# Sigmoid attention and hypermixer: stores by token group over 128 partitions, and the last column half in two PSUM banks

## The chip, the cores and the metric

The kernel runs on one core of a Trainium2 chip. TensorE (PE) multiplies matrices and writes PSUM; VectorE (DVE) and ScalarE (ACT) read PSUM and write SBUF; GpSimd (POOL) works on SBUF alone; SyncE (SP) issues nearly all DMA transfers, which 16 DMA engines carry out. The metric is the time of one execution on the device, in microseconds; lower is better.

## What is computed

```python
# q, k, v: (8 sequences, 12 heads, 448 tokens, 64), float32
scores = scale * q @ k.T - log(448)
attn   = 1 / (1 + exp(-scores))              # sigmoid, no softmax
x      = (attn @ v), heads side by side      # (8, 448, 768)
wq, wk = x @ w_q, x @ w_k                    # (8, 448, 64) each
W_tok  = scale * wq @ wk.T                   # tokens by tokens
out    = relu(W_tok @ x) @ w_out             # (8, 448, 768), float32
```

## The kernel before

The attention of a sequence is done in three groups ("quads") of four heads, so there are 24 quads. A quad's q, k and v are loaded in float32 (448 KB each), cast to bfloat16 mostly by POOL, transposed by DVE or by TensorE, and multiplied: scores on TensorE, sigmoid on ACT (L331), values on TensorE, a copy to SBUF on DVE (L355). After three quads the sequence goes through the token mixer, whose last product with w_out gives rows of the output. A string written out by hand, PLAN, sets the order of all steps; its letters S and P are scores and values, O and o a part of an output block, D lets one waiting block of output be stored. A second string, BANKS, names for each step the PSUM bank or pair of banks that it takes: PSUM has eight banks, in four pairs numbered 0 to 3.

Token t of a sequence is numbered t = 7 p + i, p from 0 to 63 and i from 0 to 6. A token group is one i: 64 tokens, which lie 7 rows apart in the output. Each row of the output has 768 floats, in two column halves of 384.

Output is made in three ways, by the pair w of sequences to which it belongs.

- `out_chunk`, for w = 0 and 1: 128 partitions hold two token groups, 64 partitions each, all 768 columns. The store (L649 to L652) is two transfers, one for each half of the partitions: 64 partitions, 3072 bytes each, 192 KB.
- `out_pair`, for w = 2 and 3, one sequence at a time: partitions 0 to 63 hold the first column half and partitions 64 to 127 the second one, of token groups k and k + 4, which stand side by side in the tile `o` as `o[:, 0]` and `o[:, 1]`. The store (L604 to L610) is two transfers, one for each half of the partitions, that is for each column half: 64 partitions, 2 x 1536 bytes each, 192 KB. The block of w = 2 that holds the middle group of both sequences goes out in four transfers of 32 partitions (L612 to L616).
- `middle`, for the middle group (i = 3) of the two sequences of w = 3, which is the last block of the program: partitions 0 to 63 are the one sequence's tokens, 64 to 127 the other's. Its four parts are the first and the second three of the six blocks of the sum, for column half 0 and then for column half 1. Each column half has one bank of a pair; when it is complete, DVE copies its columns 0 to 191 and then ACT its columns 192 to 383 (L555), out of the same bank. ACT's copy waits for DVE's. Half 0 is stored in one transfer, half 1 in two of 64 partitions, on SP's queue and on ACT's (L559).

SP issues its transfers in program order. Each transfer raises one of eight counters, in turn, when it has landed, and the next one on the same counter waits for that; so at most eight are under way. The float32 loads share six buffers (`lds`, tiles ld), and a load waits until the cast of what lay there before is done. The output blocks of w = 0, 1 and most of w = 2 lie in five buffers of their own (tile o); the last ones use the six load buffers, when no load is left.

Of the kernel before, what the change touches and what calls it, by code (L numbers as in the profile page):

```python
# [17 lines left out]
def kernel(  # L18
# [12 lines left out]
    nc = tc.nc  # L31
    B, H, S, HD = q.shape
    D = H * HD
# [3 lines left out]
    NI, NP = 7, 64  # L37
    NU = B
    NJ = H // 4
    NC = D // P  # L40
    NB = D // 2
    HALF = (slice(0, 64), slice(64, 128))
# [5 lines left out]
    def pool(name, bufs, **kw):  # L48
# [20 lines left out]
        "021012h01210321g201321g2h01gh201g20132cd302c302302131e301230"  # L69
        "ef310ef3102102c302d320d320123cd20gh120g102310g102hg102312gh1"  # L70
        "0210ef130210ef1302120120320312321031021021321a31032032132012"
        "0123020210320120c3210210312"
    )
    given = list("".join(BANKS))
    held = set()
# [1 line left out]
    def bank2():  # L77
        n = int(given.pop(0))
        assert not held & {2 * n, 2 * n + 1}
        held.update({2 * n, 2 * n + 1})  # L80
        return n, pairs[n], pairs16[n]

    def bank1():
        b = "abcdefgh".index(given.pop(0))
        assert b not in held
        held.add(b)
        return "abcdefgh"[b], pairs[b // 2][:, b % 2], pairs16[b // 2][:, b % 2]

    def release(fb):
        gone = {2 * fb, 2 * fb + 1} if isinstance(fb, int) else {"abcdefgh".index(fb)}  # L90
        assert gone <= held
        held.difference_update(gone)

    wout16 = singles.tile([P, 2 * NC, D], BF16, name="wout16")
# [14 lines left out]
    def ld_next():  # L109
        nld[0] += 1  # L110
        return lds[(nld[0] - 1) % 6]
# [8 lines left out]
    def mm(*args, **kw):  # L120
        products.append(nc.tensor.matmul(*args, **kw))  # L121
# [6 lines left out]
    COPY = dict(v=nc.vector.tensor_copy, s=nc.scalar.copy, g=nc.gpsimd.tensor_copy)  # L128
# [387 lines left out]
    ot = {}  # L516
# [4 lines left out]
    def flush(n=None):  # L521

        for _, f in stores[:n]:
            f()
        del stores[:n]

    def o_tile(shape):

        while stores and stores[0][0] <= o_tiles[0] - 5:
            flush(1)  # L530
        o_tiles[0] += 1
        return p_o.tile(shape, F32, tag="o", name="o")

    def slot(half, b):

        return b // 2 + (0 if b % 2 == half else NC)

    def middle(w, us, k, part, fb, ps):

        x = part // 2  # L540
        for c in range(part % 2 * NC // 2, (part % 2 + 1) * NC // 2):
            for u in us:
                st = mxs[w].rearrange("p (c u s) -> p c u s", u=2, s=S)[:, c, u, 3 * NP : 4 * NP]
                mm(
                    ps[HALF[u], x, 0:NB], st, wout16[:, c, x * NB : (x + 1) * NB],
                    start=(c == 0), stop=(c == NC - 1),
                )
        if part % 2:
            if not x:
                ot[0] = ld_next()[:, 0:D]  # L550
            o = ot[0][:, x * NB : (x + 1) * NB]
            half = NB // 2
            for y in range(2):
                cols = slice(y * half, (y + 1) * half)
                COPY["vs"[y]](out=o[:, cols], in_=ps[:, x, cols])  # L555
            rows = out[2 * w : 2 * w + 2].rearrange("u (p i) d -> (u p) i d", i=NI)[:, NI // 2, x * NB : (x + 1) * NB]
            if x:
                for y in range(2):
                    (nc.sync, nc.scalar)[y].dma_start(out=rows[HALF[y]], in_=o[HALF[y]])  # L559
            else:  # L560
                nc.sync.dma_start(out=rows, in_=o)
        if part < 3:
            opened.append((w, us, k, part + 1, fb, ps))
        else:
            release(fb)

    def out_pair(act, tail):

        if opened:
            w, us, k, part, fb, ps = opened.pop()  # L570
        else:
            w, us, k = chunks.pop(0)
            part = 0
            fb, ps, _ = bank2()
        if len(us) == 2 and w == MIXED:
            middle(w, us, k, part, fb, ps)
            return
        mx = mxs[w].rearrange("p (b s) -> p b s", b=12)
        at = S // 2 - 32 if len(us) == 2 else k * NP + (32 + S // 2 if us[0] else 0)
        for b in range(3 * part, 3 * part + 3):  # L580
            for y in range(2):
                st = mx[HALF[y], b, at : at + NP]
                if w == MIXED:
                    j = (b - b % 2) * S + us[0] * S + (b % 2) * 4 * NP + k * NP
                    st = mxs[w][HALF[y], j : j + NP]
                for x in range(2):
                    mm(
                        ps[HALF[x], y, 0:NB], st, wout16[HALF[y], slot(y, b), x * NB : (x + 1) * NB],
                        start=(b == 0), stop=(b == 11),
                    )  # L590
        if part < 3:
            opened.append((w, us, k, part + 1, fb, ps))
            return
        late = len(cast) == len(ORDER) + 2
        ends = w == NU // 2 - 1 and us[-1] and len(chunks) < 2
        o = ld_next()[:, 0:D].rearrange("p (b x) -> p b x", b=2) if late else o_tile([P, 2, NB])
        if ends:
            for y in range(2):
                COPY["vs"[y]](out=o[:, y], in_=ps[:, y, 0:NB])
        else:  # L600
            COPY["s" if act else "v"](out=o, in_=ps[:, :, 0:NB])
        release(fb)

        def store():  # L604
            for x in range(2):
                cols = slice(x * NB, (x + 1) * NB)
                if len(us) == 1:
                    (nc.scalar if ends and x else nc.sync).dma_start(
                        out=out[2 * w + us[0]].rearrange("(p i) d -> p i d", i=NI)[:, k : k + 5 : 4, cols], in_=o[HALF[x]],
                    )  # L610
                    continue
                for u in us:  # L612
                    nc.sync.dma_start(
                        out=out[2 * w + u].rearrange("(r n i) d -> i n r d", r=2, i=NI)[NI // 2, :, :, cols],
                        in_=o[64 * x + 32 * u : 64 * x + 32 * u + 32],
                    )  # L616

        stores.append((o_tiles[0] - 1, store))
        if tail or late:
            flush()  # L620

    def out_chunk(act, tail):

        if opened:
            w, m, nb, fb, ps = opened.pop()
            part = 1
        else:
            w, m, nb = chunks.pop(0)
            if nb < 0:
                nb = 0  # L630
                chunks.insert(0, (w, m, 1))
            fb, ps, _ = bank1()
            part = 0
        if nb == 0 and not part:
            ot[0] = o_tile([P, D])
        o = ot[0]
        ps = ps if part else ps[:, 0:NB]
        for c in range(part * NC // 2, (part + 1) * NC // 2):
            mm(
                ps, mxs[w][:, 2 * S * c + m * P : 2 * S * c + (m + 1) * P],  # L640
                wout16[:, c, nb * NB : (nb + 1) * NB], start=(c == 0), stop=(c == NC - 1),
            )
        if not part:
            opened.append((w, m, nb, fb, ps))
            return
        COPY["s" if act else "v"](out=o[:, nb * NB : (nb + 1) * NB], in_=ps)  # L646
        release(fb)

        def store():  # L649
            for y in range(2):  # L650
                b, i = divmod(2 * m + y, NI)
                nc.sync.dma_start(out=out[2 * w + b].rearrange("(p i) d -> p i d", i=NI)[:, i], in_=o[HALF[y]])  # L652

        if nb:
            stores.append((o_tiles[0] - 1, store))
# [23 lines left out]
    def cols(r):  # L679
        return slice(r.start * HD, r.stop * HD)  # L680
# [8 lines left out]
        out=ident, in_=ident, compare_op=ALU.not_equal, fill=1.0, base=0,  # L689
# [93 lines left out]
    for t16, t32, r, e in (  # L783
# [3 lines left out]
            out=t16[:, r].rearrange("p i b d -> p b i d"),  # L787
            in_=t32[:, :, cols(r)].rearrange("p b (i d) -> p b i d", d=HD),
# [3 lines left out]
    def tr_part(nm, t16, r, e, tiled=False):  # L792
# [19 lines left out]
        out=k016[:, K3].rearrange("p i b d -> p b i d"), in_=k0[:, :, cols(K3)].rearrange("p b (i d) -> p b i d", d=HD),  # L812
# [10 lines left out]
    for t in PLAN:  # L823
        pump_loads()
        pump()
        if t in "EF":
            fb, ps, _ = bank2()
# [13 lines left out]
        c = done[kind]  # L841
# [4 lines left out]
        elif kind == "P":  # L846
            n, i = divmod(c, NI)
# [15 lines left out]
        elif t == "z":  # L863
            n = quads_r.pop(0)
# [12 lines left out]
        elif kind == "C":  # L877
            for y in range(2):
                nc.sync.dma_start(
                    out=wout16[HALF[y], NC + 2 * c : NC + 2 * c + 2, :], in_=wout16[HALF[1 - y], 2 * c : 2 * c + 2, :],  # L880
# [5 lines left out]
        elif kind == "M":  # L886
            u, x = divmod(c, NC // 2)
# [42 lines left out]
```

## Time and profile before

| | |
|---|---|
| median of 3 runs (lowest, highest) | 185.74 us (184.32, 186.18) |
| the profiled execution's own time | 185.85 us |
| its span, first to last instruction | 184.1 us |
| mean granted TensorE clock | 0.995 |
| bytes read from HBM, written | 35.78 MB, 11.01 MB |
| first and last output transfer issued | 69.97 us, 180.45 us |
| last TensorE work on the chain ends | 179.68 us |

How to read it: a busy share is the part of the span in which an engine had an instruction under way. In the windows, the column after the granted clock (PEclk) is the mean busy share of the 16 DMA engines, and the last one the GB/s that they moved. SPq and ACTq are the issues of transfers from SP's and ACT's queue; the time of an issue is that of the queue, not of the transfer. The chain of waits is followed back from the last instruction, at each step to what released it.

### The profile page before, as it was taken

How to read it: one execution, taken by the hardware profiler on the slowest of the kernel's cores; microseconds unless marked ns; L12 is line 12 of the kernel's file. 1: busy time of each engine (PE TensorE's matmuls, PEld its weight loads, DVE VectorE, ACT ScalarE, POOL GpSimd, SP SyncE). 2: the span in 40 equal slices, each digit the busy share in tenths (PEclk: the TensorE clock that was granted, in tenths of full speed). 3: DMA queues.
4: the chain of work that ended last, by engine and by line, in shares of the span. 5: the costliest groups of instructions: out<-in, count | busy, mean ns of one | idle time of the engine just before them, and what ended most of it. 6: DMA issues, size and time to landing. Idle time of an engine off the chain costs nothing.

```text
span 184.1 us, 8404 instructions
## 1 busy us (share of the span) xinstructions
PE 171.2 (93%) x3618; PEld 112.3 (61%) x3618; DVE 134.0 (73%) x205; ACT 159.9 (87%) x207; POOL 117.0 (64%) x156
## 2 busy tenths in 40 slices
PE   7987778799999999999999999999999999999990
PEld 7544434454564655565656556456778898888970
DVE  2445679988999898988848877689785894694310
ACT  4699998999999999998998999999989979974330
POOL 1445696999799996799999937999999400000000
PEclk9999999999999999999999999999999999999998
DMA  5999999968999768999979998998992343432686
GB/s 176 370 382 283 305 356 333 394 244 267 400 395 390 226 215 272 353 270 366 338 199 309 313 335 271 325 391 286 303 313 65 90 111 90 109 90 66 148 223 172
DMA packets 24261, 48.51 MB, mean 264 GB/s; under 512 B 3872, under 2 KB 16416, under 8 KB 24224
## 3 DMA queue, kind: packets, MB, share of 16 engines
q1 hardware_dynamic: 24000, 47.69, 79.3%
q8 instruction: 28, 0.46, 1.0%
q10 hardware_dynamic: 224, 0.30, 0.6%
q14 instruction: 9, 0.07, 0.1%
HBM read 35.78 MB, written 11.01 MB: 254 GB/s over the span
## 4 chain that ended last, share of the span: by engine, by line
PE 80%; DVE 5%; ACT 5%; issue 3%; POOL 2%; DMA 2%; SPq 0%; ACTq 0%; POOLq 0%
PE banks L121 76%; PE banks L124 4%; ACT at L331 4%; DMA ld<-in_moe_w_k_dram 2%; DVE xt L355 1%; POOL wqk L754 1%; DVE qk L251 1%; POOL qk L211 1%; DVE qk L264 1%; DVE mx L469 1%; POOL v L221 0%; DVE k L221 0%; DVE xn L384 0%; DVE wqk L429 0%; ACT qk L801 0%
## 5 line engine op out<-in xcount | busy, mean ns | idle before, releaser
L331 ACT ACTIVATE at<-banks 128x896 bf16<-128x896 f32 x168 | 141.6, 940 | 6.6 <-PE banks L121 6.1
L121 PE MATMUL banks<-wout,mx 64*64 64x384 bf16 (+2 forms) x816 | 66.2, 324 | 0.7 <-issue 0.6
L121 PE MATMUL banks<-qk 64*64 64x448 bf16 x672 | 60.8, 358 | 4.2 <-ACT at L331 2.7
L121 PEld LDWEIGHTS <-mx 64*64 64x64 bf16 (+2 forms) x816 | 39.5, 105 | 17.5 <-issue 7.1
L211 POOL CAST qk<-ld 128x896 bf16<-128x896 f32 x38 | 44.6, 1193 | 8.4 <-issue 7.2
L121 PE MATMUL banks<-at,v 64*64 64x448 bf16 x672 | 46.7, 350 | 1.5 <-POOL v L221 0.8
L121 PEld LDWEIGHTS <-qk 64*64 64x64 bf16 x672 | 26.6, 105 | 24.8 <-issue 18.0
L355 DVE CAST xt<-banks 128x896 bf16<-128x896 f32 x23 | 25.0, 1086 | 7.6 <-PE banks L121 5.8
L121 PEld LDWEIGHTS <-v 64*64 64x64 bf16 x672 | 23.3, 106 | 7.5 <-issue 1.5
L469 DVE TENSOR_SCALAR mx<-banks 128x896 bf16<-128x896 f32 (+1 forms) x21 | 19.9, 955 | 5.0 <-PE banks L121 4.2
L221 POOL CAST v<-ld 128x896 bf16<-128x896 f32 x22 | 20.3, 930 | 1.2 <-DMA ld<-in_v_dram 0.6
L271 DVE STREAM_TRANSPOSE qk<-qk 128x448 f32<-128x448 f32 x26 | 16.0, 629 | 0.1
L251 DVE STREAM_TRANSPOSE qk<-qk 32x448 f32<-32x448 f32 x24 | 15.3, 636 | 0.6
L384 DVE COPY xn<-banks 128x896 bf16<-128x896 bf16 x21 | 13.1, 624 | 3.6 <-PE banks L124 2.6
L170 POOL COPY qk<-qk 32x448 uint32<-32x448 uint32 x26 | 14.4, 554 | 1.6
L173 POOL COPY qk<-swap 32x448 uint32<-32x448 uint32 x26 | 14.4, 554 | 1.5
L121 PE MATMUL banks<-xt,wqk 64*64 64x448 bf16 (+1 forms) x84 | 13.8, 353 | 0.2 <-ACT at L331 0.2
L646 DVE COPY o<-banks 128x384 f32<-128x384 f32 x17 | 9.4, 553 | 3.4 <-PE banks L121 3.0
L124 PEld LDWEIGHTS <-xt 64*64 64x64 bf16 (+1 forms) x588 | 9.8, 108 | 3.1 <-issue 1.6
L124 PE MATMUL banks<-ident,xt 64*64 64x64 bf16 (+1 forms) x588 | 10.4, 194 | 0.2
L121 PE MATMUL banks<-wqk,tmp 64*64 64x448 bf16 (+3 forms) x72 | 8.7, 291 | 0.0
L121 PE MATMUL banks<-wq,tmp 64*64 64x448 bf16 (+2 forms) x72 | 8.4, 292 | 0.0
(67 smaller groups left out, 136.1 us busy)
## 6 DMA issues: line engine op xcount, KB each, us to landing
ld<-in_q_dram SPq DMA_DIRECT2D x24, 448.0 KB, 6.1
ld<-in_v_dram SPq DMA_DIRECT2D x24, 448.0 KB, 5.9
ld<-in_k_dram SPq DMA_DIRECT2D x23, 448.0 KB, 5.9
out_dram<-o SPq DMA_DIRECT2D x38, 192.0 KB, 4.9
out_dram<-ld SPq DMA_DIRECT2D x14, 192.0 KB, 3.0
ld<-in_moe_w_out_dram SPq DMA_DIRECT2D x6, 384.0 KB, 5.3
wout<-wout SPq DMA_DIRECT2D x6, 192.0 KB, 5.7
out_dram<-o SPq DMA_DIRECT2D x4, 96.0 KB, 1.9
```

The source lines that it names most:

```text
L121: products.append(nc.tensor.matmul(*args, **kw))
L124: products.append(nc.tensor.transpose(*args, **kw))
L170: eng.tensor_copy(out=w[lo, 1], in_=w[hi, 0])
L173: eng.tensor_copy(out=w[hi, 0], in_=z[lo])
L211: COPY[e](out=f[:, :, "qk".index(nm)].rearrange("p e i d y -> p e y i d"), in_=ld.pop((nm, n)).rearrange("p (y i e d) -> p e y i d", y=2, ...
L221: COPY[e](out=t16.rearrange("p i b d -> p b i d"), in_=ld.pop((nm, n)).rearrange("p b (i d) -> p b i d", i=NI),)
L251: nc.vector.transpose(out=qk[n][other : other + 32, h].rearrange("p t i n -> p (t i n)").bitcast(F32), in_=w[own : own + 32, 1 - h],)
L271: nc.vector.transpose(out=qk[n][:, t].rearrange("p t i n -> p (t i n)").bitcast(F32), in_=w)
L331: nc.scalar.activation(dst, src, ACTF.Sigmoid, bias=attn_bias, scale=attn_scale)
L355: COPY[eng](out=xt(u, j), in_=ps)
L384: COPY[eng](out=xn, in_=ps)
L469: nc.vector.tensor_scalar(dst, ps, moe_scale, 0.0, ALU.mult, ALU.max)
```

## The change

Four things change.

- `out_chunk`: where both token groups of a block belong to the same sequence, one transfer of 128 partitions and 384 KB stores it. The pattern of its destination has the token group outermost (2), then the tokens (64), then 768 columns. One block in seven has its two groups in different sequences; its two transfers stay.
- `out_pair`, one sequence at a time: the two transfers are now one for each token group, `o[:, 0]` and `o[:, 1]`, each of 128 partitions and 192 KB. The pattern of the destination has the column half outermost (2), then the tokens (64), then 384 columns.
- `middle`: column half 0 is copied by DVE alone. Column half 1 is made as two pieces of 192 columns, each over all six blocks of the sum, in the two banks of another pair (number 0, the one added to BANKS). DVE copies the first piece, ACT the second. The transfers of the block are the same.
- In the last but one block, each of the two stores needs one of the two copies (DVE's for `o[:, 0]`, ACT's for `o[:, 1]`), where each needed both.

```diff
--- before.py
+++ after.py
@@ -69,7 +69,7 @@
         "021012h01210321g201321g2h01gh201g20132cd302c302302131e301230"
         "ef310ef3102102c302d320d320123cd20gh120g102310g102hg102312gh1"
         "0210ef130210ef1302120120320312321031021021321a31032032132012"
-        "0123020210320120c3210210312"
+        "0123020210320120c32102103120"
     )
     given = list("".join(BANKS))
     held = set()
@@ -537,32 +537,35 @@
 
     def middle(w, us, k, part, fb, ps):
 
-        x = part // 2
-        for c in range(part % 2 * NC // 2, (part % 2 + 1) * NC // 2):
+        if part < 2:
+            begin, n, cs = 0, NB, range(part * NC // 2, (part + 1) * NC // 2)
+        else:
+            begin, n, cs = (part * NB // 2, NB // 2, range(NC))
+        if part == 2:
+            release(fb)
+            fb, ps, _ = bank2()
+        for c in cs:
             for u in us:
                 st = mxs[w].rearrange("p (c u s) -> p c u s", u=2, s=S)[:, c, u, 3 * NP : 4 * NP]
                 mm(
-                    ps[HALF[u], x, 0:NB], st, wout16[:, c, x * NB : (x + 1) * NB],
+                    ps[HALF[u], part // 3, 0:n], st, wout16[:, c, begin : begin + n],
                     start=(c == 0), stop=(c == NC - 1),
                 )
-        if part % 2:
-            if not x:
-                ot[0] = ld_next()[:, 0:D]
-            o = ot[0][:, x * NB : (x + 1) * NB]
-            half = NB // 2
-            for y in range(2):
-                cols = slice(y * half, (y + 1) * half)
-                COPY["vs"[y]](out=o[:, cols], in_=ps[:, x, cols])
-            rows = out[2 * w : 2 * w + 2].rearrange("u (p i) d -> (u p) i d", i=NI)[:, NI // 2, x * NB : (x + 1) * NB]
-            if x:
-                for y in range(2):
-                    (nc.sync, nc.scalar)[y].dma_start(out=rows[HALF[y]], in_=o[HALF[y]])
-            else:
-                nc.sync.dma_start(out=rows, in_=o)
+        if not part:
+            ot[0] = ld_next()[:, 0:D]
+        o = ot[0]
+        if part:
+            COPY["s" if part == 3 else "v"](out=o[:, begin : begin + n], in_=ps[:, part // 3, 0:n])
+        cols = slice(0, NB) if part < 2 else slice(NB, D)
+        rows = out[2 * w : 2 * w + 2].rearrange("u (p i) d -> (u p) i d", i=NI)[:, NI // 2, cols]
+        if part == 1:
+            nc.sync.dma_start(out=rows, in_=o[:, cols])
         if part < 3:
             opened.append((w, us, k, part + 1, fb, ps))
-        else:
-            release(fb)
+            return
+        for y in range(2):
+            (nc.sync, nc.scalar)[y].dma_start(out=rows[HALF[y]], in_=o[HALF[y], cols])
+        release(fb)
 
     def out_pair(act, tail):
 
@@ -602,13 +605,14 @@
         release(fb)
 
         def store():
+            if len(us) == 1:
+                for y in range(2):
+                    (nc.scalar if ends and y else nc.sync).dma_start(
+                        out=out[2 * w + us[0]].rearrange("(p i) (x c) -> i x p c", i=NI, x=2)[k + 4 * y], in_=o[:, y],
+                    )
+                return
             for x in range(2):
                 cols = slice(x * NB, (x + 1) * NB)
-                if len(us) == 1:
-                    (nc.scalar if ends and x else nc.sync).dma_start(
-                        out=out[2 * w + us[0]].rearrange("(p i) d -> p i d", i=NI)[:, k : k + 5 : 4, cols], in_=o[HALF[x]],
-                    )
-                    continue
                 for u in us:
                     nc.sync.dma_start(
                         out=out[2 * w + u].rearrange("(r n i) d -> i n r d", r=2, i=NI)[NI // 2, :, :, cols],
@@ -647,6 +651,10 @@
         release(fb)
 
         def store():
+            b, i = divmod(2 * m, NI)
+            if i + 1 < NI:
+                nc.sync.dma_start(out=out[2 * w + b].rearrange("(p i) d -> i p d", i=NI)[i : i + 2], in_=o)
+                return
             for y in range(2):
                 b, i = divmod(2 * m + y, NI)
                 nc.sync.dma_start(out=out[2 * w + b].rearrange("(p i) d -> p i d", i=NI)[:, i], in_=o[HALF[y]])
```

In what follows a row is one instruction, or several alike with their count; for a transfer the numbers are the counts of the destination's pattern, the outermost first. Names: ld_101 and the like are load buffers, o a block of output, wout_83 the bfloat16 weights, banks PSUM.

SP's queue at the first stores of output, at 70 us of the span before:

```order
 L197 DMA ld_102<-in_v_dram 128x2x448
-L652 DMA out_dram<-o 64x768 x4
-L879 DMA wout_83<-wout_83 64x1536 x2
-L652 DMA out_dram<-o 64x768 x2
+L656 DMA out_dram<-o 2x64x768 x2
+L887 DMA wout_83<-wout_83 64x1536 x2
+L656 DMA out_dram<-o 2x64x768
 L189 DMA ld_103<-in_k_dram 128x896
 L189 DMA ld_104<-in_q_dram 128x896
```

Nothing changes its place: six stores of 64 partitions become three of 128, ahead of the same two loads, and the outermost count goes from 64 to 2.

SP's queue where the output blocks change from `out_chunk` to `out_pair` (from 130 us before). Before:

```order
L652 DMA out_dram<-o 64x768 x6
L608 DMA out_dram<-o 64x2x384 x6
L613 DMA out_dram<-o 32x2x384 x4
L608 DMA out_dram<-o 64x2x384 x4
L608 DMA out_dram<-ld_101 64x2x384 x2
```

After, the same place:

```order
L656 DMA out_dram<-o 2x64x768 x3
L610 DMA out_dram<-o 2x64x384 x6
L617 DMA out_dram<-o 32x2x384 x4
L610 DMA out_dram<-o 2x64x384 x4
L610 DMA out_dram<-ld_101 2x64x384 x2
```

The transfers stand in the same order; the stores by token group are as many as those by column half were, with 2 outermost in place of 64.

ACT's queue at the end of the program:

```order
-L599 COPY ld_101<-banks 128x384
-L608 DMA out_dram<-ld_101 64x2x384
-L555 COPY ld_102<-banks 128x192 x2
-L559 DMA out_dram<-ld_102 64x384
-L925 UNCONDITIONAL_BRANCH
+L604 COPY ld_104<-banks 128x768
+L604 COPY ld_100<-banks 128x768
+L602 COPY ld_101<-banks 128x384
+L610 DMA out_dram<-ld_101 2x64x384
+L558 COPY ld_102<-banks 128x192
+L567 DMA out_dram<-ld_102 64x384
```

ACT has one copy of 192 columns in the last block where it had two.

## The prediction

> **What bounds the kernel now.** I read the page first: busy shares, slices, the chain.
>
> ```profile
> PE 171.2 (93%) x3618; PEld 112.3 (61%) x3618; DVE 134.0 (73%) x205; ACT 159.9 (87%) x207; POOL 117.0 (64%) x156
> ...
> PEclk9999999999999999999999999999999999999998
> DMA  5999999968999768999979998998992343432686
> ...
> PE 80%; DVE 5%; ACT 5%; issue 3%; POOL 2%; DMA 2%; SPq 0%; ACTq 0%; POOLq 0%
> ```
>
> TensorE is the bound: 93% busy, 80% of the chain that ended last, at full granted clock. Second are the 16 DMA engines: 9 in nearly every slice up to three quarters of the span, then 2 to 4, then up again. Next I cut the run where the first output is stored, and cut out short stretches in which the transfers are of one shape.
>
> ```profile
> core 0: us, PE busy (x) PEld busy (x) DVE busy (x) ACT busy (x) POOL busy (x), PEclk, DMA share, GB/s
> 56.00:60.00 4.00, 4.00 (x40) 1.59 (x44) 3.84 (x6) 4.00 (x7) 3.63 (x7) 1.00 1.00 383
> 134.00:134.75 0.75, 0.75 (x33) 0.59 (x29) 0.75 (x2) 0.62 (x2) 0.75 (x2) 1.00 1.05 397
> 142.00:142.50 0.50, 0.50 (x23) 0.30 (x19) 0.39 (x1) 0.50 (x2) 0.44 (x2) 1.00 0.94 190
> 150.50:152.25 1.75, 1.75 (x50) 1.72 (x45) 1.08 (x2) 1.68 (x3) 0.00 (x0) 1.00 0.86 205
> 181.50:182.00 0.50, 0.00 (x0) 0.00 (x0) 0.00 (x0) 0.00 (x0) 0.00 (x0) 1.00 0.80 277
> ...
> 70.00:110.00 40.00, 40.00 (x699) 22.59 (x696) 33.13 (x50) 38.66 (x53) 32.71 (x44) 1.00 0.95 307
> 110.00:135.00 25.00, 25.00 (x491) 15.80 (x493) 19.82 (x31) 23.56 (x30) 22.08 (x29) 1.00 0.93 318
> 135.00:184.10 49.10, 44.08 (x1183) 38.23 (x1172) 27.42 (x43) 33.26 (x47) 9.71 (x15) 0.98 0.49 126
> ```
>
> The last two columns carry everything below: share of the 16 engines, and bytes moved. From 70 to 135 us the engines are 93 to 95% taken and TensorE never idle: no room for more engine time there. Loads alone (56 to 60 us) give 383 / 16 / 1.00 = 23.9 GB/s per engine; the 3072-byte pieces (134.00 to 134.75, all engines full) 397 / 16 = 24.8. A store of 64 partitions and 2 x 1536 bytes each (142.0) keeps 0.94 of the engines busy and yet moves only 190 GB/s, half of a load.
>
> That last row is what the change aims at. The Trainium skill, "SBUF — State Buffer", section "Door 1: The DMA port swizzle", says that 64 partitions reach only 8 of 16 ports and measures 196 GB/s for them; the trace agrees with 190.
>
> **The change, part by part.** What is queued from the first store on, and where SP's own waits end:
>
> ```profile
> out_dram<-o SPq DMA_DIRECT2D x38, 192.0 KB, 4.9
> ld<-in_v_dram SPq DMA_DIRECT2D x11, 448.0 KB, 5.9
> ld<-in_k_dram SPq DMA_DIRECT2D x10, 448.0 KB, 6.1
> ld<-in_q_dram SPq DMA_DIRECT2D x9, 448.0 KB, 6.3
> out_dram<-ld SPq DMA_DIRECT2D x14, 192.0 KB, 3.0
> wout<-wout SPq DMA_DIRECT2D x6, 192.0 KB, 5.7
> out_dram<-o SPq DMA_DIRECT2D x4, 96.0 KB, 1.9
> out_dram<-ld ACTq DMA_DIRECT2D x1, 192.0 KB, 3.8
> out_dram<-ld SPq DMA_DIRECT2D x1, 96.0 KB, 2.6
> out_dram<-ld ACTq DMA_DIRECT2D x1, 96.0 KB, 2.7
> ```
>
> ```profile
> 69.97 3.05 SPq L652 DMA_DIRECT2D out_dram<-o  x4
> ```
>
> ```profile
> SPq L189 <- POOL qk L211: 9.3, 7, 3.6
> SPq L197 <- POOL qk L211: 8.7, 6, 3.9
> ```
>
> The first answer is the DMA view from 69 us to the end (KB of each, median us to landing), the second SP's time line, the third SP's waits from 66 to 135 us.
>
> Step 1, fewer issues. Of the 28 stores of L652, 24 become 12 of 384 KB (4 stay, where the two halves fall in different sequences). Four issues take 3.05 us, so SP saves about 12 x 0.76 = 9 us. SP waits for POOL's casts, not for itself: worth nothing; between 0 and 1 us gained, I take 0.
>
> Step 2, the shape of the stores. This is the step that I think decides. The order (quoted in the section on the change) shows patterns with the outermost count first: 128, 64 or 32 for every transfer before, 2 for the 12 merged stores and the 24 by token group. The windows show those old counts filling the engines: loads with 128 rows share 1.00, 64 rows 0.94, 32 rows 0.86 (150.50 to 152.25). So each row of the trace agrees with whole outer rows dealt over the engines, 8, 4 or 2 to each. A transfer with two outer rows then has one row for each of two engines and nothing for fourteen. No row has a count under 16, so the trace bounds the price from both sides only: at best 16 engines at 383 GB/s, at worst two engines at 2 x 23.9 = 48 GB/s. I take two, because splitting an outer row is what no row of this trace shows.
>
> The Trainium skill, "DMA: Bandwidth & Descriptors", section "Why a DMA increments its semaphore by 16 and not by 1", says the number of engines is the largest up to 16 that divides the slowest dimension of both patterns, and that they are the lowest-numbered ones; by that rule these 36 stores get two engines, the same two each time. No transfer before has a slowest count below 32, so no run here shows it yet.
>
> Price with two engines: a merged store has 393 KB, so each engine carries 196.6 KB, at 24.8 GB/s (3072-byte pieces) 7.93 us; a store by token group carries 98.3 KB per engine, at 23.9 GB/s 4.11 us. If the two are the same for all 36 stores, these two engines are a queue of their own, through which a sixteenth of every load must go as well, in order. Work of one of them from 70 us on:
>
> - 12 merged stores x 7.93 = 95.2 us
> - 24 stores by token group x 4.11 = 98.7 us
> - 30 loads of 448 KB (28.7 KB per engine, at 24.8) x 1.16 = 34.7 us
> - the rest at full width: 4 + 6 + 2 + 2 transfers' worth of 192 KB (kept halves, wout copies, the 96-KB pieces and the last block's stores), each 12.3 KB per engine = 0.51 us, together 7.2 us
>
> Sum 235.8 us. The engines are 95% taken at 70 us, so this queue begins without a gap: 70 + 236 = 306 us for the last data. Before, these 36 stores' share was 197 KB x 36, plus 12 more, over sixteen engines and lay under TensorE's work; that cover is gone, since TensorE has only about 109 us to do after 70 us.
>
> What waits then: SP's loads behind three merged stores (the first order fence) get their sixteenth on those engines some 24 us late; POOL's casts wait for them, DVE's transposes for POOL, the scores on TensorE for DVE. Later the out tiles are taken until their stores have landed, and the copies that refill them hold their PSUM banks. These waits lie inside the 236 us, beside the queue, not on top.
>
> Step 3, the last column half. Rows for the matmuls by shape, the time line's end and the chain's last pieces:
>
> ```profile
> L121 PE MATMUL banks<-xn,wkn 64*64 64x192 bf16 x196 | 5.5, 243 | 0.0
> ...
> L121 PE MATMUL banks<-wout,mx 128*64 128x384 bf16 x24 | 2.1, 328 | 0.0
> ```
>
> ```profile
> 177.60 0.56 DVE L599 COPY ld<-banks 128x384 f32<-128x384 f32 x1 [2.83 <-PE banks L121]
> ...
> 180.45 0.52 ACTq L559 DMA_DIRECT2D out_dram<-ld  x1
> ```
>
> ```profile
> 179.71 0.37 DVE ld L555
> 180.07 0.02 issue
> 180.10 0.32 ACT ld L555
> ```
>
> 12 matmuls of 384 columns become 24 of 192: the same columns, half of the 2.1 us, 1.05. The 192-column row runs four at a time, 5.5 / 49 = 112 ns a four; if a pair took as long as a four, 12 pairs would need 1.34 us, 0.3 more. I take 0, the columns being the same, and keep 0.3 as the bad end. DVE's copy of the first half is now 384 wide, 0.56 us, and lies beside the first 12 small matmuls (0.5 us); its 192-wide copy, 0.37 us, beside the other 12. ACT no longer waits for DVE behind the last matmul: 0.37 + 0.02 = 0.39 us less. It counts only if the end still hangs on that copy; behind a queue of stores it is worth 0.
>
> Sum: last data 306 us; the last transfer now is issued at 180.45, lands 2.7 us later, and the span ends at 184.1, so 0.95 us follows: 307 us of span. The profiled execution took 185.85 us, 1.75 more than its span, and the median of the runs is 185.74: no correction. **308.5 us.**
>
> **The rivals.** A, all sixteen engines work on these stores. For it: the row of 142.0 says that 64 partitions are the slow part, and the L561 store of 128 partitions (181.5: 277 GB/s at 0.80) is faster. Against it: it needs outer rows split. Then stores hide under TensorE as before, and only the end gains: 0.39 us of copies, and about 0.7 us of landing (2.6 to 2.7 now, against 1.9 for the 96-KB stores that meet no other): 185.7 - 1.1 = 184.6 us. This is the rival on the other side, not slower; it decides at 16 engines, and even then it stays under 1%. The Trainium skill, "SBUF — State Buffer", section "Door 1: The DMA port swizzle", asks for 128 partitions; taken alone it would give this time.
>
> B, two engines for a store, but another pair each time. Then loads meet a store only now and then, and the end is what shows: the last two stores by token group need 4.1 us of data instead of about 1, so the last landing moves by some 3 us: 188.5 us. Nothing in the trace speaks for it or against.
>
> C, two engines, always the same, and the waits do not overlap: each time TensorE starves, no store is made, and the queue runs dry. At most as much as the loads' share again, 35 us: 343 us. Against it: SP issues ahead of the engines, and stores pile up at the end when no load is left.
>
> The price of one engine's byte is the other open size: with the slowest full-width row (181.5, 277 / 16 / 0.80 = 21.6 GB/s) for the small pieces the sum grows by 10 us; if an engine is a tenth faster without fourteen neighbours, it falls by 18.
>
> **How the numbers follow.** Two fixed engines, as forecast: 0.76. C, the same with a queue that runs dry: 0.10, ending mostly below 340. A: 0.10. B: 0.04. The predicted time is the forecast's, 308.5 us. Its range is 290 (a tenth faster) to 340 (slow small pieces, most of C): it holds about 0.82, and leaves A, B and the far end of C outside. About 1% is what a measurement of this kernel can tell. Slower by over 1%: forecast, C and B, 0.90. Within 1%: most of A, 0.09. Faster by over 1% would need 1.9 us from an end that has 1.1 to give: 0.01.
>
> **What would show it.** In the profile after: DMA share near 2/16, 0.1 to 0.2, wherever no load runs, at some 48 GB/s; landing times of the new stores of tens of us in place of 4.9 and 3.0; POOL waiting for loads from about 80 us on, and gaps on TensorE; the last matmul well ahead of the end, by 50 us or more, with nothing but stores behind it. Step 3 is right if ACT's last copy starts within 0.1 us of the last matmul's end. I am wrong if the 2x64 stores move 300 GB/s or more at a share near 1: then A holds. If they move 48 GB/s while loads land as before, B holds.

## The result and the profile after

The changed kernel takes 303.0 us (302.5 to 305.3, 6 runs), against 186.4 us for the kernel before (184.3 to 187.1): ratio 1.630, 95% interval 1.621 to 1.639. The profiled execution took 302.69 us, its span is 300.9 us. The page's lines on the engines, the slices and the chain:

```profile
PE 184.7 (61%) x3630; PEld 118.3 (39%) x3630; DVE 133.8 (44%) x205; ACT 161.0 (54%) x206; POOL 117.2 (39%) x156
...
PEclk9999999999999569975869799799799955555555
DMA  7999989976437797114384831111131111111111
GB/s 222 385 300 385 385 260 378 324 237 215 96 119 240 248 262 264 51 52 144 130 294 127 309 114 54 54 54 50 52 101 55 50 50 50 50 50 50 61 73 51
...
DMA 43%; PE 19%; ACT 9%; SPq 9%; POOL 4%; DVE 3%; issue 2%; ACTq 0%; DVEq 0%; POOLq 0%
```

The chain has moved from TensorE (80%) to DMA (43%). The bytes are the same 48.51 MB, but in most slices without a load the DMA digit is 1 and the rate 50 to 55 GB/s: two of sixteen engines. (It is 61 to 101 where stores of the old form fall in as well.) The digit is nowhere 0, to the end: something was always in the queue. Cut where the matmuls end:

```profile
core 0: us, PE busy (x) PEld busy (x) DVE busy (x) ACT busy (x) POOL busy (x), PEclk, DMA share, GB/s
70.00:110.00 40.00, 26.61 (x414) 14.51 (x413) 20.66 (x32) 25.77 (x34) 22.24 (x30) 0.84 0.64 197
...
190.00:235.00 45.00, 35.55 (x904) 30.29 (x905) 18.79 (x31) 22.45 (x31) 0.55 (x1) 0.93 0.18 61
235.00:300.90 65.90, 1.53 (x32) 1.17 (x27) 1.47 (x3) 0.80 (x2) 0.00 (x0) 0.54 0.15 54
```

TensorE, never idle from 70 to 110 us before, works 26.6 of these 40 us, and in the last 65.9 us it has 1.5 us of matmuls. Who waited, from the view of waits (us in total, times, longest):

```profile
ACT at L331 <- PE banks L121: 52.5, 33, 13.0
POOL v L221 <- DMA ld<-in_v_dram: 27.9, 5, 21.5
...
ACT ld L602 <- DMA out_dram<-ld: 18.6, 1, 18.6
DVE o L604 <- DMA out_dram<-o: 17.7, 4, 5.7
PE banks L121 <- DVE xt L355: 17.5, 3, 13.4
ACT ld L558 <- DMA out_dram<-ld: 16.8, 1, 16.8
```

POOL waits for loads, once for 21.5 us, and the engines behind it wait in turn; behind another of these waits, of 14.4 us, TensorE stands still for 13.4 us; DVE and ACT wait for stores to land before they may fill an output buffer again.

The number of engines can be counted. Besides its data, each transfer leaves one piece of 4 bytes for each engine that took part: the trace of the kernel before has 2336 of them, 16 for each of its 146 transfers. The page counts all pieces under 512 bytes, before and after:

```profile
DMA packets 24261, 48.51 MB, mean 264 GB/s; under 512 B 3872, under 2 KB 16416, under 8 KB 24224
```

```profile
DMA packets 23565, 48.51 MB, mean 161 GB/s; under 512 B 3176, under 2 KB 15720, under 8 KB 23528
```

Before, 146 x 16 = 2336, and the loads of w_q and w_k have 2 x 6 x 128 = 1536 pieces of 256 bytes: 3872. After there are 134 transfers. If each of the 36 new stores takes two engines, it is 98 x 16 + 36 x 2 + 1536 = 3176, the number on the page.

### The profile page after: what moved, and what is told of

Read it like the earlier page. It is cut to its first block, busy times and chain, and to the rows that moved or that the text cites. A ratio compares the mean times of both kernels' runs of the same rounds, so it can differ in the third digit from the quotient of the medians.

```text
span 300.9 us, 8407 instructions
## 1 busy us (share of the span) xinstructions
PE 184.7 (61%) x3630; PEld 118.3 (39%) x3630; DVE 133.8 (44%) x205; ACT 161.0 (54%) x206; POOL 117.2 (39%) x156
## 2 busy tenths in 40 slices
DMA packets 23565, 48.51 MB, mean 161 GB/s; under 512 B 3176, under 2 KB 15720, under 8 KB 23528
## 4 chain that ended last, share of the span: by engine, by line
DMA 43%; PE 19%; ACT 9%; SPq 9%; POOL 4%; DVE 3%; issue 2%; ACTq 0%; DVEq 0%; POOLq 0%
DMA out_dram<-o 22%; PE banks L121 18%; DMA out_dram<-ld 10%; ACT at L331 9%; DMA ld<-in_q_dram 6%; DMA ld<-in_k_dram 4%; SPq L610 3%; SPq L197 2%; SPq L656 2%; POOL qk L211 2%; PE banks L124 1%; SPq L189 1%; POOL qk L173 1%; DVE o L604 1%; POOL qk L170 1%
## 5 line engine op out<-in xcount | busy, mean ns | idle before, releaser
L121 PE MATMUL banks<-qk 64*64 64x448 bf16 x672 | 64.8, 379 | 37.1 <-DVE xt L355 13.6
L121 PE MATMUL banks<-wout,mx 64*64 64x384 bf16 (+3 forms) x828 | 70.8, 343 | 8.5 <-DVE o L604 4.5
L121 PEld LDWEIGHTS <-mx 64*64 64x64 bf16 (+2 forms) x828 | 41.9, 112 | 28.7 <-issue 18.0
L121 PE MATMUL banks<-at,v 64*64 64x448 bf16 x672 | 50.1, 369 | 0.7 <-ACT at L331 0.6
L121 PEld LDWEIGHTS <-v 64*64 64x64 bf16 x672 | 24.2, 112 | 7.6 <-issue 1.3
L170 POOL COPY qk<-qk 32x448 uint32<-32x448 uint32 x26 | 14.4, 554 | 1.6
L173 POOL COPY qk<-swap 32x448 uint32<-32x448 uint32 x26 | 14.4, 554 | 1.5
L121 PE MATMUL banks<-xt,wqk 64*64 64x448 bf16 (+1 forms) x84 | 14.4, 361 | 0.2 <-ACT at L331 0.2
L604 DVE COPY o<-banks 128x768 f32<-128x768 f32 x6 | 5.7, 956 | 18.1 <-DMA out_dram<-o 17.7
L650 ACT COPY o<-banks 128x384 f32<-128x384 f32 x11 | 5.4, 493 | 9.6 <-DMA out_dram<-o 9.0
```

What stands on the lines that cost most here:

```text
L170: eng.tensor_copy(out=w[lo, 1], in_=w[hi, 0])
L173: eng.tensor_copy(out=w[hi, 0], in_=z[lo])
```

## The experiments

The first four tell which part of the change costs what, and whether it is the outermost count. Each ran beside the kernel before (185.65 us).

**The last column half alone.** The whole of the diff's `middle` and BANKS, and the stores as before.

> Only the last column half is changed (two banks of 192 columns, one copy each); all stores as before. Theory, that the 117 us come from the outermost count of 2 alone: about 0.4 us less than before (the copy that waited for the other engine, 0.37 + 0.02 us), so a ratio of 0.998. Rival, that the 24 small matmuls take 0.3 us more: 0.1 us less. If this part carried some of the loss, it would be slower than before.

Measured: 185.58 us, ratio 0.9989 (0.9959 to 1.0020): no difference that can be told. The time line (start and duration in us) shows that the step does what it says:

```profile
176.76 3.61 PE L121 MATMUL banks<-wout,mx 64*64 64x384 bf16 x68
...
179.47 0.82 DVE L558 COPY ld<-banks 128x384 f32<-128x384 f32 x2 [0.63 <-PE banks L121]
...
180.41 0.32 ACT L558 COPY ld<-banks 128x192 f32<-128x192 f32 x1 [1.60 <-DMA out_dram<-ld]
```

DVE's two copies (x2) end at 180.29. The matmuls end at 176.76 + 3.61 = 180.37, and ACT's copy begins 0.04 us later; it no longer has a copy of DVE ahead of it in its bank. (The page names an earlier store of the output buffer as what ended ACT's wait; the last matmul ends as close to it, and the row can't part the two.) The matmuls by shape took 1.2 us for the 24 small ones, as for the 12 of 384 columns:

```profile
L121 PE MATMUL banks<-wout,mx 128*64 128x384 bf16 x12 | 1.2, 330 | 0.0
L121 PE MATMUL banks<-wout,mx 128*64 128x192 bf16 x24 | 1.2, 246 | 0.0
```

So this part carries none of the loss, and the bad end of 0.3 us for the matmuls did not come.

**The merged stores alone.**

```diff
         def store():
+            b, i = divmod(2 * m, NI)
+            if i + 1 < NI:
+                nc.sync.dma_start(out=out[2 * w + b].rearrange("(p i) d -> i p d", i=NI)[i : i + 2], in_=o)
+                return
             for y in range(2):
```

> Only the stores of out_chunk are merged (12 transfers of 384 KB, outermost count 2). Theory, two fixed engines through which the loads pass too: before the last load 11 or 12 stores of 7.7 us (64 pieces of 0.121 us) stand in that queue, with the loads' 35 us and some 7 us of the rest, so the last load lands near 185 to 195 us instead of 135, and the 49 us that followed it before follow again: 230 to 245 us. Rival, another pair of engines for each store: within 3 us of before.

Measured: 239.53 us, ratio 1.290 (1.281 to 1.298), in the theory's range. SP's time line has the last load:

```profile
172.91 0.33 SPq L189 DMA_DIRECT2D ld<-in_q_dram  x1
```

Before, this load was issued at 129.36 us; it comes 43.5 us later, so most of the loss came through the loads. The rest did not follow as before, as the theory had it: the span goes on for 63.8 us behind this issue, where it was 54.7. In this stretch DVE waits 10.4 us, in three waits, for stores to land before it may fill their buffers again; in the kernel before it has no such wait there. The last load came sooner than expected, too (POOL's last cast of a load ends at 183.7 us, where the landing was put at 185 to 195), so the two errors cancelled in part.

**The token-group stores alone.**

```diff
         def store():
+            if len(us) == 1:
+                for y in range(2):
+                    (nc.scalar if ends and y else nc.sync).dma_start(
+                        out=out[2 * w + us[0]].rearrange("(p i) (x c) -> i x p c", i=NI, x=2)[k + 4 * y], in_=o[:, y],
+                    )
+                return
             for x in range(2):
...
```

> Only the stores of out_pair go by token group (24 transfers of 192 KB, outermost count 2). Theory, two fixed engines: no load is behind them but the last few, so TensorE ends near 180 us as before, and the queue runs from 135 us on for 24 x 4.16 us = 100 us: last landing near 237, time 238 to 242 us. Rival, that the loss of both parts comes through the waiting loads: within a few us of before.

Measured: 237.28 us, ratio 1.277 (1.269 to 1.286), 0.7 us below the stated 238 to 242: an engine was a little quicker than I had put it (below). The windows:

```profile
135.00:180.00 45.00, 44.63 (x1212) 39.17 (x1204) 26.97 (x41) 32.84 (x45) 10.61 (x16) 1.00 0.23 79
180.00:236.50 56.50, 0.00 (x0) 0.00 (x0) 1.27 (x3) 1.02 (x3) 0.00 (x0) 0.53 0.15 55
```

TensorE ran as before up to 180 us, 44.63 of 45.00 us busy; then 56 us of nothing but stores at 55 GB/s. The same two engines cost the first part through the loads and this part at the end. Alone the parts add 53.9 and 51.6 us, 105.5 in sum; together they add 116.6 (303.0 against the 186.4 beside it). No run divides the other 11 us. They fit the order of the queue: in the changed kernel the first three token-group stores take 19.5 us to be issued, from 185.3 us on, behind the last merged ones.

**The same stores with 64 outermost.** From the changed kernel:

```diff
-out=out[2 * w + us[0]].rearrange("(p i) (x c) -> i x p c", i=NI, x=2)[k + 4 * y], in_=o[:, y],
+out=out[2 * w + us[0]].rearrange("(p i) (x c) -> i p x c", i=NI, x=2)[k + 4 * y], in_=o[:, y],
...
-nc.sync.dma_start(out=out[2 * w + b].rearrange("(p i) d -> i p d", i=NI)[i : i + 2], in_=o)
+nc.sync.dma_start(out=out[2 * w + b].rearrange("(p i) d -> p i d", i=NI)[:, i : i + 2], in_=o)
```

> The changed kernel, with the two dimensions of the merged and of the token-group destinations exchanged, so that 64 stands outermost: the same transfers, bytes, piece sizes and 128 source partitions, but the pieces land in each other's places in the output. Theory, that the outermost count sets the number of engines: 16 engines again, 184.5 to 186 us. Rival, that reading 128 partitions at once, or long merged transfers, is what is slow: 303 us again.

Measured: 184.79 us, ratio 0.9960 (0.9930 to 0.9989). (Its pieces land in the wrong places of the output, so it is a measure and no candidate.) The order of two dimensions of the destination is worth 118 us. The page's pieces, and a window in which the last stores run:

```profile
DMA packets 24069, 48.51 MB, mean 265 GB/s; under 512 B 3680, under 2 KB 16224, under 8 KB 24032
```

```profile
179.50:180.50 1.00, 0.08 (x2) 0.00 (x0) 0.01 (x1) 0.32 (x1) 0.00 (x0) 1.00 1.03 367
```

134 x 16 + 1536 = 3680: all on sixteen engines. And 367 GB/s at full share, from 128 partitions. The 190 GB/s of the kernel before (142.0) is not its fair opposite: that is the first store of a pair, and the end of the same pair, also from 64 partitions each, moved more than the loads did (383):

```profile
142.75:143.00 0.25, 0.25 (x16) 0.23 (x8) 0.24 (x1) 0.25 (x2) 0.23 (x1) 1.00 1.09 393
```

By the pieces of the trace, a whole pair took 1.79 us before (from 141.64 us) and 1.32 us with 64 outermost (from 142.09 us), a quarter less and not half. Rival A's price, 184.6 us, was right; only its condition was not met.

Why does a count of 2 mean two engines? Whole rows dealt out as far as they go, as I had read it from the trace, and the largest divisor up to 16, as the Trainium skill has it, agree on 2, 32, 64 and 128. The next runs take counts on which they differ, in the kernel before, by cutting each `out_pair` store in two (beside a kernel before of 186.05 us); N is 32, 51 and 62:

```diff
-(nc.scalar if ends and x else nc.sync).dma_start(
-    out=out[2 * w + us[0]].rearrange("(p i) d -> p i d", i=NI)[:, k : k + 5 : 4, cols], in_=o[HALF[x]],
-)
+for r in (slice(0, N), slice(N, 64)):
+    (nc.scalar if ends and x else nc.sync).dma_start(
+        out=out[2 * w + us[0]].rearrange("(p i) d -> p i d", i=NI)[r, k : k + 5 : 4, cols],
+        in_=o[64 * x + r.start : 64 * x + r.stop],
+    )
```

> The kernel before, with each out_pair store of 64 partitions cut into two of 32 and 32: control for the next two. Both theories give 16 engines to an outermost count of 32; 24 more issues of 0.43 us on SP hide. 185 to 187 us.

> The same, cut into 51 and 13 partitions. Theory of the largest divisor up to 16: 51 = 3 x 17 goes over 3 engines, 17 rows x 2 pieces x 65 ns = 2.2 us each, 13 over 13 engines (0.13 us); 24 stores need 56 us of the lowest three engines from 135 us on, with little room for gaps: 194 to 203 us. Rival, that whole outer rows are dealt over all 16 engines as far as they go: 51 rows are 4 to an engine, so as the control, 185 to 187 us.

> The same, cut into 62 and 2 partitions. Theory of the largest divisor up to 16: 62 = 2 x 31 goes over two engines, 31 x 2 x 0.065 = 4.03 us each, and 2 over two, 0.13 us: 24 x 4.16 = 100 us of the same two engines, 236 to 243 us, as with the token-group stores alone (237.3). Rival, whole outer rows dealt over 16 engines: 185 to 187 us. This tells which of the two makes an outermost count of 2 slow, the small count or the divisor.

Measured: 185.67 us, ratio 0.9994 (0.9950 to 1.0037), for 32; 200.36 us, 1.077 (1.069 to 1.085), for 51 and 13; 237.32 us, 1.275 (1.265 to 1.285), for 62 and 2. The pieces of 51 and 13, then those of 62 and 2:

```profile
DMA packets 24261, 48.51 MB, mean 244 GB/s; under 512 B 3872, under 2 KB 16416, under 8 KB 24224
```

```profile
DMA packets 23973, 48.51 MB, mean 207 GB/s; under 512 B 3584, under 2 KB 16128, under 8 KB 23936
```

Of 170 transfers, 122 take 16 engines. With 51 and 13: 122 x 16 + 24 x 3 + 24 x 13 + 1536 = 3872. With 62 and 2: 122 x 16 + 48 x 2 + 1536 = 3584. Both numbers are the page's. (The first is that of the kernel before, since 3 + 13 = 16; there the count alone shows nothing, and the time and the rate must.) Of 62 rows 16 engines could take nearly four each, and two engines take them all. In the last stretch of each, with no load and few other stores under way:

```profile
184.00:198.00 14.00, 0.00 (x0) 0.00 (x0) 0.00 (x0) 0.54 (x2) 0.00 (x0) 0.50 0.32 98
```

```profile
190.00:230.00 40.00, 0.00 (x0) 0.00 (x0) 0.62 (x2) 0.54 (x2) 0.00 (x0) 0.50 0.15 57
```

98 GB/s with 3 (and now and then 13) engines, 57 with two (the block of the program's end adds some stores on sixteen to both). The Trainium skill, "DMA: Bandwidth & Descriptors", section "Why a DMA increments its semaphore by 16 and not by 1", states this rule, and that the lowest-numbered engines are taken. These runs show the rule at 2, 51, 13 and 62. The times and the share of 0.13 to 0.15, while more stores wait, show that it is the same two engines each time; which numbers they have, no view here shows.

**A version that might beat both.** The middle as in the first experiment, and the `out_pair` stores in 32-partition pieces, the halves in turn:

```diff
+if len(us) == 1:
+    for r in (slice(0, 32), slice(32, 64)):
+        for x in range(2):
+            (nc.scalar if ends and x else nc.sync).dma_start(
+                out=out[2 * w + us[0]].rearrange("(p i) d -> p i d", i=NI)[r, k : k + 5 : 4, x * NB : (x + 1) * NB],
+                in_=o[64 * x + r.start : 64 * x + r.stop],
+            )
+    return
...
```

> The last column half as in the change, and each out_pair store in four transfers of 32 partitions, the first and the second 64 partitions in turn, so that both halves are under way together. If the slow first store of a pair (190 to 206 GB/s) comes from its 64 partitions alone, the end gains 0.3 to 0.7 us over the middle alone: 184.9 to 185.4 us. Rival, that four issues of 0.43 us take longer than they save at the end: 185.5 to 186.5 us.

Measured: 185.53 us beside 186.05, ratio 0.9969 (0.9938 to 1.0001). As it stands this is just within the rival's range; but the kernel before, beside it, is 0.4 us slower than beside the middle alone, so the times do not decide. The trace does: from 145.50 to 147.25 us the four stores of a block move 206 GB/s, no more than the 32-partition stores of the kernel before (205 at 150.50). Taking the halves in turn did not make them faster. This version is far faster than the changed kernel, and not shown to be faster than the kernel before. The 0.4% that the stores with 64 outermost gain stays out of reach for one transfer with a right layout: with the tile as it is, the partitions run over the column halves first, and so must the destination.

## Why the prediction was right

The forecast was 308.5 us, the time is 303.0. By its steps:

- Step 1, fewer issues, worth 0: it could not show. What came instead is that issues became long (last section).
- Step 2, two fixed engines for 36 stores, is the cause: both parts alone cost their share, exchanging two dimensions takes it all back, and the pieces counted on the page fit two engines for each of the 36. My reason from the trace was the wrong one of two that agreed: I had taken whole rows as dealt out as far as they go, and 62 rows show that the divisor counts. For a count of 2 both give the same, so that reading led to the right number by luck.
- The size: the sum had 235.8 us of queue and a gapless start at 70 us. Two terms were too large. The first is the 24 stores by token group, put at 23.9 GB/s per engine and 4.11 us each. A window in which they run alone, in the changed kernel:

```profile
240.00:264.00 24.00, 0.00 (x0) 0.00 (x0) 1.47 (x3) 0.48 (x1) 0.00 (x0) 0.51 0.13 50
```

50 GB/s over two engines is 25 each, 3.93 us a store: 24 x 0.18 = 4.3 us less. The 23.9 had come from a stretch of loads of two piece sizes; the price of an engine alone is 5% better, inside the tenth that the range allowed. The second is the 12 merged stores, put at 24.8 and 7.93 us: where they run alone (128 to 131 us) the two engines move 52 GB/s, 26 each, so about 7.6 us a store and some 4 us less. Together that is some 8 us, and the forecast was 5.5 too long: about 2.5 us the other way are in no term, and no run here says where.
- Rival C, a queue that runs dry while TensorE starves, did not come: no slice's DMA digit falls to 0 and its rate never below 50 GB/s.
- Rival A had the right price (184.6; 184.8 measured with 64 outermost) and the wrong condition. Rival B, another pair of engines each time, would have made some 3 us of it; either part alone cost over 50.
- Step 3 was taken as worth 0.39 us only where the end hangs on the copy. In the changed kernel it does not: ACT's last copy waited 16.8 us for a store of the buffer it fills. Alone it is below what can be told.
- Of the signs named, the DMA share (0.13 to 0.18), POOL's waits for loads, and matmuls that end some 64 us early came; the landing times cannot be read, since the profile of the changed kernel gives none, for its loads neither.

## What to carry to other kernels

Read the destination's and the source's pattern of each transfer from the outermost dimension that is not 1, and see which is the largest number up to 16 that divides both counts: that is how many DMA engines it gets. (The runs show it with the destination's count, and with both alike; none has a small count in the source alone.) A store that covers all 128 partitions is worth nothing if the other side begins with a dimension of 2; if the order cannot be turned, two transfers of 64 partitions are better, as in the kernel before. And price a transfer on few engines by the queue that it makes there, since every later load needs its share of those engines too.

## What the runs showed that I had not expected

An issue is not always short. SP's issues of the new stores, from the changed kernel's view of that line (min/median/max in ns):

```profile
L610 SPq DMA_DIRECT2D out_dram<-ld x13: 3223/3807/6745, 233.2 to 283.6; - x13
L610 SPq DMA_DIRECT2D out_dram<-o x10: 521/3775/8322, 185.3 to 229.3; - x10
```

Before, the same issues took 0.6 us. With two engines behind, an issue takes about as long as a store's data (median 3.8 us, beside 3.93), so SP itself stops, with all that stands behind it. Its time line has the issue of one load that took 7.8 us, where loads elsewhere take 0.33:

```profile
79.95 7.80 SPq L189 DMA_DIRECT2D ld<-in_k_dram  x1
```

TensorE's granted clock falls in long stretches in which it has nothing to do: 0.51 from 240 to 264 us, with no matmul, and 0.54 over the last 65.9 us, against 0.995 before. From 106 to 110 us, after its wait of 13.4 us, it is 0.50 although TensorE is busy for 3.45 of the 4 us. Its busy time rose from 171.2 to 184.7 us, for only 12 matmuls more. No slice shows the queue of the two engines running dry meanwhile, so no cost of it is seen here.
